# W2 steps take the block stored first, and the emission clock counts PSUM banks

## The chip, the cores and the metric

One core of a Trainium2 chip. The metric is the device time of one execution in microseconds (us). Ratios are the mean time of one kernel's fast runs over that of the other's fast runs of the same rounds, so they are not quite the ratio of the medians quoted beside them.

## The reference, cut to what matters

Two layers; each adds a sliding-window attention and a gated feed-forward block to x (2048 rows of 1024):

```python
x = x + attention(layernorm(x), wqkv, wo)          # 32 heads, 8 keys at distance 2
h = silu(layernorm(x) @ w1) * (layernorm(x) @ w3)  # 3584 columns
x = x + h @ w2
# both lines twice, with the same weights
```

## The kernel before: the parts concerned

The work is cut in eight units: layer, and chunk of 512 rows. The first two units compute the feed-forward block plainly. From the third on, w1, w3 and w2 products use a scheme of seven half-size products, P1 to P7, in place of eight. It needs sums of weight blocks. ScalarE copies and scales four blocks, VectorE makes three more by additions and subtractions, POOL stores all seven to DRAM; there are two blocks for this, 0 and 1, in the buffer `big`. There are two blocks for this, in one buffer (`big`).

```python
big = const.tile([P, 7168], FP16, name="big")
sums = big[:, 0:3072]...                      # norm sums of the activations, for P5, P6, P3
snaps = [big[:, 3072 + 1024 * i: ...]...]     # four snapshots of products
blocks = [big[:, 3584 * i:3584 * (i + 1)]... for i in range(2)]   # block 0 lies over sums
```

A step for W2, as the program is written out (`yield "blocked"` puts the step off):

```python
def sums_of_w2(i, f, ws, loaded):
    a = f % 2
    while "at" not in got2 or pending[a]:
        yield "blocked"
    pending[a] += 1
    ...  # four ScalarE copies into block a; four VectorE operations; pending[a] -= 1; POOL stores block a
    stored[a] = now["dve"] + 7.0
```

The order of instructions on every engine is fixed while the program is written out, by a clock that estimates when each engine gets to what. Fill-in work is put in where the clock says that there is room:

```python
def act_background():                      # ScalarE's fill-in: norms, sizes, sums
    for queue in (acts, sizes, parts, reads):
        while True:
            s = head(queue)
            if s is None or max(now["act"], s[1]) + s[0] > now["pe"] + gate[0]:   # gate is 2.2 us
                break
            take_act(queue)
```

Of the kernel before, what the change touches and what calls it, by code (L numbers as in the profile page):

```python
# [17 lines left out]
def kernel(  # L18
# [137 lines left out]
    opened = [0]  # L156

    def side_tile(*args, **kw):

        while opened[0]:  # L160
            assert head(makes) is not None
            take(makes)
        return side.tile(*args, **kw)

    def bank(name):
        if name == "po":
            return side_tile([P, 512], FP32, name=name, tag="sd")
        return psum.tile([P, 512], FP32, name=name, tag="mm")
# [49 lines left out]
    size_v = const.tile([P, 4], FP32, name="size_v")  # L218
    down_v = const.tile([P, 1], FP32, name="down_v")
    up_v = const.tile([P, 1], FP32, name="up_v")  # L220
# [6 lines left out]
    blocks += [hT[:, 9:16, :].bitcast(FP16).rearrange("p b (k c) -> p b k c", k=KT // 2)]  # L227
    t2_d = [dram.tile([P, 7, (b - a) // 2, 512], FP16, name=f"t2_d{i}") for i, (a, b) in enumerate(fsplits)]
    t_d = [[dram.tile([P, 14, KT // 2, P], FP16, name=f"t_d{m}_{g}") for g in range(NG)] for m in range(2)]
    t_d += [[dram.tile([P, 14, KT // 2, P], FP16, name=f"t_dv_{g}") for g in range(2)]]  # L230
# [350 lines left out]
    def score_steps():  # L581

        V = nc.vector
        for g, (l, h) in enumerate(halves):
# [20 lines left out]
            def gather_heads(t, parts_=parts_):  # L605
                at["L"] = L = side_tile([P, W, BLK], FP32, name="L", tag="sd")
                for i in range(parts_):
                    for a in range(4):
                        nc.tensor.matmul(L[32 * a:32 * (a + 1), :, :], lhsT=gather[:],
                                         rhs=psm[:, :, i, a * BLK:(a + 1) * BLK], start=i == 0, stop=i == parts_ - 1,  # L610
                                         skip_group_check=True)
                at["t"] = pe(1.5 * parts_, t) + 0.2
# [19 lines left out]
            def exps():  # L632
                V.tensor_tensor(L[:], L[:], mx[:].unsqueeze(1).to_broadcast([P, W, BLK]), op=ALU.subtract)
                nc.scalar.activation(E[:], L[:], ACTF.Exp, scale=scale)
                at["E"] = act(0.65, now["dve"] + 0.1, "exp")

# [123 lines left out]
    def o_tile():  # L760
# [12 lines left out]
        for hh in range(2):  # L773
            ps = bank("po")
            for t in range(KT):
                nc.tensor.matmul(ps[:], lhsT=oT[:, t, j * P:(j + 1) * P], rhs=wo[:, t, hh * 512:(hh + 1) * 512],  # L776
                                 start=(t == 0), stop=(t == KT - 1))
            r = pe(KT, oT_at[l, h] + 0.2)
            xs = x_sb[:, n, hh * 512:(hh + 1) * 512]
            background(r)  # L780
            nc.vector.tensor_tensor(xs, xs, ps[:], op=ALU.add)  # L781
            dve(0.64, r)
# [42 lines left out]
    def q_part(l, c, which, ws, then=()):  # L825
# [8 lines left out]
        for t0 in range(0, KT, SG):  # L834
# [3 lines left out]
            for t in range(t0, t0 + SG):  # L838
                ps = bank("ps")
                for kk in range(KT):  # L840
                    nc.tensor.matmul(ps[:], lhsT=ws[kk // KH][:, kk % KH, t::KT], rhs=xnT[:, kk, :],  # L841
                                     start=(kk == 0), stop=(kk == KT - 1))
# [4 lines left out]
                if first:  # L847
                    nc.scalar.copy(kT[:, t, HALO:], ps[:, 0:TCH])
                    done = act(0.3)
                if t < t0 + SG - 1:  # L850
                    pe_requests(2)
            nc.sync.dma_start(qkv_d[l][which][:, t0:t0 + SG, c * CH:(c + 1) * CH], sgt)
            landed = dma(256, done)
            if l == 0:
                stored[0:2] = landed, landed
# [47 lines left out]
    def weight_sums(m, g, w, got):  # L903
# [4 lines left out]
        for a in range(2):  # L908
# [9 lines left out]
            makes.append([differences(m, g, a, a, now["act"] + 0.1), None])  # L918
        made.add((m, g))

    pending, stored, made, held = [0] * 3, [0.0] * 3, set(), []
    junk = hsum[:].bitcast(BF16).rearrange("p k t -> p (k t)")

    def differences(m, g, a, slot, r):

        b = blocks[slot]
# [3 lines left out]
        pending[slot] -= 1  # L930
        nc.gpsimd.dma_start(t_d[m][g][:, 4 * a:4 * (a + 1)], b[:, 0:4])
        nc.gpsimd.dma_start(t_d[m][g][:, 8 + 3 * a:8 + 3 * (a + 1)], b[:, 4:7])
        stored[slot] = now["dve"] + 7.0

    got_v = {}

    def size_of_v(i, w):

        w_ = w[:].rearrange("p k c -> p (k c)")
        half = w_.shape[1] // 2  # L940
        for j in range(2):
            yield 1.95, 40.0, lambda: nc.scalar.activation(junk, w_[:, j * half:(j + 1) * half], ACTF.Square,
                                                           accum_out=size_v[:, 2 * i + j:2 * i + j + 1])
        if i == 1:
            total_scale(size_v, up_v, down_v, got_v)

    def sums_of_v(ws):

        while "at" not in got_v or norm_left.get(("Q", 0, NCH - 1), 1):
            yield "blocked"  # L950
        for g in range(2):
            for a in range(2):
                while pending[2]:
                    yield "blocked"
                pending[2] += 1
                b = blocks[2]
                for i, (kh, fh) in ((0, (0, 0)), (1, (0, 1)), (3, (1, 0)), (5, (1, 1))):
                    t = 4 * g + 2 * fh + a
                    yield 0.61, max(got_v["at"], stored[2]) + 1.0, lambda: nc.scalar.activation(
                        b[:, i], ws[kh][:, :, t::KT], ACTF.Copy, scale=up_v[:])  # L960
                makes.append([differences(2, g, a, 2, now["act"] + 1.0), None])
        made.add("v")
# [72 lines left out]
    def sums_of_w2(i, f, ws, loaded):  # L1035

        a = f % 2
        while "at" not in got2 or pending[a]:
            yield "blocked"
        pending[a] += 1  # L1040
# [28 lines left out]
    def pipeline(key, groups, consume, done, last, fill=None):  # L1069
# [6 lines left out]
        def acc():  # L1076
            return psum.tile([P, 2, HT], FP32, name="st", tag="mm")
# [12 lines left out]
        def head_part(i, name):  # L1090
            G = groups[i]
            s5, su, s22 = snaps[i % 2], snaps[2], snaps[3]
            if name == "P1":
                G["early"] = weight("early")
                G["A"] = acc()
                r = run(G, name, G["A"], True)
                G["B"] = acc()
                nc.scalar.copy(G["B"][:], G["A"][:])  # L1098
                G["tB"] = act(0.5, r)
            elif name == "P5":  # L1100
                G["D"] = acc()
                r = run(G, name, G["D"], True)
# [9 lines left out]
            elif name == "P2":  # L1112
                r = run(G, name, G["B"], False, G["tB"])
                release(1)
                consume(G, 0, G["B"][:], r)
# [11 lines left out]
            elif name == "P3":  # L1127
                r = run(G, name, G["D"], False, G["tD"])
                consume(G, 1, G["D"][:], r)
            else:  # L1130
                r = run(G, name, G["A"], False, G["tC"])
                release(1)
                consume(G, 2, G["A"][:], r)
# [19 lines left out]

    def v_products(l, c):

        key = ("Q", l, c)
        slots, landed = [0], []

        def stage(G, pair):
            if ("to", pair) not in G:  # L1160
                i = slots[0] % 8 * SG
                slots[0] += 1
                G["to", pair] = hT[:, i:i + SG, :]
                G["left", pair] = 2
            return G["to", pair]

        def consume(G, q, src, r):
            pair, t0 = q % 2, HT * (q // 2)
            to = stage(G, pair)
            if q != 3:  # L1170
                nc.scalar.activation(to[:, :, t0:t0 + HT], src, ACTF.Copy, scale=down_v[:])
                r = act(0.57, r)
            G["left", pair] -= 1
            G["at", pair] = max(r, G.get(("at", pair), 0.0))
            if not G["left", pair]:
                t = 4 * G["g"] + 2 * pair
                nc.sync.dma_start(qkv_d[l][2][:, t:t + SG, c * CH:(c + 1) * CH], to)
                landed.append(dma(256, G["at", pair]))
                if len(landed) == 4:
                    qkv_at[l, c, 2] = max(landed)  # L1180

        groups = []
        for g in range(2):
            G = dict(m=2, g=g, inv=down_v[:])
            G["corner"] = lambda G=G: stage(G, 1)[:, :, HT:CH]
            groups.append(G)
        pipeline(key, groups, consume, lambda i: between(False, i == 0), True)
        xnT_free[key] = now["pe"]

    def products(u, f0, f1, hold):  # L1190
# [25 lines left out]
        def output(j, hh, src, r):  # L1216
# [4 lines left out]
            dve(0.69, r)  # L1221
            if l == 1 and lastsplit:
                nc.sync.dma_start(xout[:, n, hh * 512:(hh + 1) * 512], xs)
                dma(128, now["dve"])

        def W(name, j):
# [12 lines left out]
            if name == "P1":  # L1239
                G["A"] = bank("w2")  # L1240
                r = G["1"] = matmuls(G["A"], True)
                G["B"] = bank("w2")
                nc.scalar.copy(G["B"][:], G["A"][:])
                G["tB"] = act(0.5, r)
            elif name == "P2":
                r = G["2"] = matmuls(G["B"], False, G["tB"])
                output(j, 0, G["B"][:], r)
            elif name == "P5":
                G["D"] = bank("w2")
                r = matmuls(G["D"], True)  # L1250
# [15 lines left out]
            elif name == "P3":  # L1266
                r = matmuls(G["D"], False, G["tD"])
                output(j, 1, G["D"][:], r)
            else:
                r = matmuls(G["A"], False, G["tC"])  # L1270
                output(2 + j, 0, G["A"][:], r)
# [20 lines left out]
        def consume(G, q, src, r):  # L1292
            m, g, f = G["m"], G["g"], G["f"] + 2 * (q % 2)
            inv = G["inv"]
            if m == 0:
                sg = gates[g, q] = sgp.tile([P, 2, HT], BF16, name="sg", tag="sg")
                nc.scalar.activation(sg[:], src, ACTF.Silu, scale=inv)  # L1297
                G["t", q] = act(0.6, r, "silu")
            else:
                if q != 3:  # L1300
                    up = tight[:, 1] if q == 2 else sgp.tile([P, 2, HT], BF16, name="up", tag="up", bufs=1)[:]
                    nc.scalar.activation(up, src, ACTF.Copy, scale=inv)
                    src, r = up, act(0.5, r)
                background(r + 0.5)
                t0 = HT * (q // 2)
                nc.vector.tensor_tensor(h16[:, f:f + 2, t0:t0 + HT], src, gates[g, q][:], op=ALU.mult)
                dve(0.34, r)

# [14 lines left out]
    def b_stage(u, hold):  # L1323
# [5 lines left out]
        for (f0, f1) in fsplits:  # L1329
# [4 lines left out]
            for g0 in range(f0, f1, FG):  # L1334
# [3 lines left out]
                for fi in range(gn):  # L1338
# [8 lines left out]
                    pg = bank("pg")  # L1347
                    for kk in range(KT):
# [5 lines left out]
                    ts = act(0.5, r, "silu")  # L1354
                    act_background()
                    pu = bank("pu")
                    for kk in range(KT):
# [5 lines left out]
                    th = dve(0.64, r)  # L1363
                    release_held(2)
# [9 lines left out]
            for hh in range(2):  # L1374
                now["pe"] = max(now["pe"], *times[hh])
                for j in range(TPC):
                    n, step = c * TPC + j, TPC * hh + j
                    acc = psum.tile([P, 512], FP32, name="acc", tag="mm")
# [13 lines left out]
                    dve(0.64, r)  # L1392
# [6 lines left out]
        if u == TU - 1:  # L1399
            force(makes, lambda: not any(pending[0:2]))  # L1400
# [82 lines left out]
```

## Time and profile before

| | before |
|---|---|
| time, median of 3 (4 at the second reading) | 1542.65 us (1542.95) |
| TensorE busy, of the span | 1521.5 of 1542.1 us |
| sum of TensorE's waits in the profile | 14.5 us |
| half-clock stretch of TensorE inside the run | 3.4 us, at 569.4 |

The lines that carry this are in the prediction.

### The profile page before, as it was taken

How to read it: one execution, taken by the hardware profiler on the slowest of the kernel's cores; microseconds unless marked ns; L12 is line 12 of the kernel's file. 1: busy time of each engine (PE TensorE's matmuls, PEld its weight loads, DVE VectorE, ACT ScalarE, POOL GpSimd, SP SyncE). 2: the span in 40 equal slices, each digit the busy share in tenths (PEclk: the TensorE clock that was granted, in tenths of full speed). 3: DMA queues.
4: the chain of work that ended last, by engine and by line, in shares of the span. 5: the costliest groups of instructions: out<-in, count | busy, mean ns of one | idle time of the engine just before them, and what ended most of it. 6: DMA issues, size and time to landing. Idle time of an engine off the chain costs nothing.

```text
span 1542.1 us, 25098 instructions
## 1 busy us (share of the span) xinstructions
PE 1521.5 (99%) x9595; PEld 990.2 (64%) x9634; DVE 1200.9 (78%) x2126; ACT 884.8 (57%) x1388; POOL 156.8 (10%) x308
## 2 busy tenths in 40 slices
PE   9999999999999999999999999999999999999999
PEld 7666644444444567675685756867677667686865
DVE  4689998889979678989898958799688986445345
ACT  3885476667465346555574554666557345554633
POOL 1210102121111100102101010010202000000000
PEclk9999999999999999999999999999999999999999
DMA  9887969798896899969879888798979988878885
GB/s 326 192 230 211 271 209 337 266 307 268 270 307 226 289 326 316 313 236 312 294 285 310 310 282 270 268 342 295 308 259 322 347 281 285 311 273 333 313 295 205
DMA packets 261433, 439.57 MB, mean 285 GB/s; under 512 B 73856, under 2 KB 201088, under 8 KB 245056
## 3 DMA queue, kind: packets, MB, share of 16 engines
q1 hardware_dynamic: 248464, 390.90, 77.2%
q0 software_dynamic: 12704, 46.93, 8.7%
q8 instruction: 75, 1.23, 0.3%
q14 instruction: 46, 0.38, 0.1%
q10 hardware_dynamic: 144, 0.13, 0.0%
HBM read 345.90 MB, written 67.90 MB: 268 GB/s over the span
## 4 chain that ended last, share of the span: by engine, by line
PE 55%; DVE 4%; DMA 3%; ACT 3%; issue 1%; POOL 1%; ACTq 0%; DVEq 0%; POOLq 0%
PE st L1086 29%; PE w L1235 15%; PE ps L841 6%; PE po L776 4%; DMA qkv_d<-hT 1%; DMA t_d<-big 1%; DMA kT<-qkv_d 1%; DVE tree L595 1%; DMA xnT<-xn 1%; DVE tree L515 1%; ACT sg L1297 0%; DVE tree L670 0%; ACT big L1043 0%; ACT xn L323 0%; ACT L1297 0%
## 5 line engine op out<-in xcount | busy, mean ns | idle before, releaser
L841 PE MATMUL ps<-xnT,wqkv 128*128 128x512 f16 (+1 forms) x1469 | 320.7, 379 | 3.1 <-ACT hT L845 1.8
L1086 PEld LDWEIGHTS <-early 128*128 128x128 f16 x2688 | 263.1, 98 | 39.9 <-DVE big L303 1.7
L841 PEld LDWEIGHTS <-wqkv 128*128 128x128 bf16 x1472 | 210.6, 144 | 111.6 <-issue 4.0
L1235 PE MATMUL w<-t,hT 128*128 128x512 f16 x1008 | 226.3, 379 | 1.5 <-ACT big L1255 1.2
L1086 PEld LDWEIGHTS <-late 128*128 128x128 f16 x2016 | 197.4, 98 | 33.8 <-issue 5.5
L595 DVE TENSOR_TENSOR tree<-qT,kT 128x2048 bf16<-128x2048 bf16 x128 | 156.2, 1221 | 29.0 <-DMA qT<-qkv_d 15.4
L670 DVE TENSOR_TENSOR tree<-At,vT 128x2048 bf16<-128x2048 bf16 x128 | 156.1, 1220 | 26.8 <-DMA At<-E 25.2
L515 DVE TENSOR_TENSOR tree<-tree 128x1024 bf16<-128x1024 bf16 x256 | 175.2, 685 | 0.9
L1086 PE MATMUL st<-big,early 128*128 128x256 f16 x1344 | 172.8, 273 | 1.9 <-DVE big L303 1.4
L1086 PE MATMUL st<-xnT,late 128*128 128x256 f16 x1344 | 174.2, 273 | 0.2
L1235 PEld LDWEIGHTS <-hT 128*128 128x128 f16 x1008 | 98.3, 98 | 113.6 <-issue 3.1
L1086 PE MATMUL st<-xnT,early 128*128 128x256 f16 x1344 | 165.3, 273 | 0.0
L1098 ACT COPY st<-st 128x512 f32<-128x512 f32 x84 | 48.3, 575 | 119.6 <-PE st L1086 118.8
L776 PE MATMUL po<-wo,oT 128*128 128x512 bf16 x487 | 111.6, 379 | 2.9 <-DVE x_sb L781 1.6
L1358 PE MATMUL pu<-xnT,w3t 128*128 128x512 f16 x448 | 105.8, 379 | 0.0
L1349 PE MATMUL pg<-xnT,w1t 128*128 128x512 f16 x448 | 105.8, 379 | 0.0
L1380 PE MATMUL acc<-w2t,hT 128*128 128x512 bf16 x437 | 97.8, 379 | 0.6
L1110 DVE TENSOR_TENSOR st<-st,big 128x512 f32<-128x512 f32 x84 | 58.4, 695 | 50.2 <-ACT big L1107 50.1
L845 ACT CAST hT<-ps 128x512 bf16<-128x512 f32 x96 | 54.9, 586 | 71.3 <-PE ps L841 70.2
L1297 ACT ACTIVATE sg<-st,down_scale 128x512 bf16<-128x512 f32 x126 | 86.7, 688 | 12.6 <-PE st L1086 12.1
L1086 PE MATMUL st<-big,late 128*128 128x256 f16 x672 | 87.9, 274 | 3.8 <-DVE st L1110 3.8
L776 PEld LDWEIGHTS <-oT 128*128 128x128 bf16 x512 | 50.0, 98 | 58.3 <-issue 2.6
(167 smaller groups left out, 1919.3 us busy)
## 6 DMA issues: line engine op xcount, KB each, us to landing
early<-t_d SPq DMA_DIRECT2D x84, 1024.0 KB, 6.9
late<-t_d SPq DMA_DIRECT2D x84, 768.0 KB, 6.4
t<-t_d SPq DMA_DIRECT2D x42, 1024.0 KB, 7.6
t<-t_d SPq DMA_DIRECT2D x42, 768.0 KB, 5.3
wqkv<-in_A_wqkv_dram SPq DMA_DIRECT2D x28, 1024.0 KB, 9.0
w1t<-in_B_w_dram SPq DMA_DIRECT2D x14, 1024.0 KB, 8.0
w3t<-in_B_w_dram SPq DMA_DIRECT2D x14, 1024.0 KB, 10.9
t_d<-big POOLq DMA_DIRECT2D x28, 512.0 KB, 6.0
```

Source lines behind the costliest of these rows:

```text
L515: nc.vector.tensor_tensor(b, b, buf[:, 4:8, :], op=ALU.add)
L595: V.tensor_tensor(pr, qT[:], kT[:, :, k0:k0 + TCH], op=ALU.mult)
L670: V.tensor_tensor(tm.rearrange("p w (a e) -> p w a e", a=4), At[:].rearrange("p a w e -> p w a e"), win, op=ALU.mult)
L776: nc.tensor.matmul(ps[:], lhsT=oT[:, t, j * P:(j + 1) * P], rhs=wo[:, t, hh * 512:(hh + 1) * 512], start=(t == 0), stop=(t == KT - 1))
L841: nc.tensor.matmul(ps[:], lhsT=ws[kk // KH][:, kk % KH, t::KT], rhs=xnT[:, kk, :], start=(kk == 0), stop=(kk == KT - 1))
L1086: nc.tensor.matmul(out[:, a, :], lhsT=w[:, a, blk, k, :], rhs=rhs[:, k, :], start=start and a == 0 and k == 0, stop=k == KQ - 1, skip_grou ...
L1110: nc.vector.tensor_tensor(G["D"][:], G["D"][:], su, op=ALU.add)
L1235: nc.tensor.matmul(out[:], lhsT=lhs[:, k, j * P:(j + 1) * P], rhs=w[:, k, :], start=start and k == 0, stop=k == nq - 1, skip_group_check=True)
L1297: nc.scalar.activation(sg[:], src, ACTF.Silu, scale=inv)
L1349: nc.tensor.matmul(pg[:], lhsT=w1t[:, kk, fi * P:(fi + 1) * P], rhs=xnT[:, kk, :], start=(kk == 0), stop=(kk == KT - 1))
L1358: nc.tensor.matmul(pu[:], lhsT=w3t[:, kk, fi * P:(fi + 1) * P], rhs=xnT[:, kk, :], start=(kk == 0), stop=(kk == KT - 1))
L1380: nc.tensor.matmul(acc[:], lhsT=hT[:, f, j * P:(j + 1) * P], rhs=tiles[hh][f // nq][:, f % nq, :], start=(f == 0), stop=(f == f1 - f0 - 1))
```

## The change

Intent: a W2 step should not wait for the block whose store was issued last when the other is free. The emission clock should also know when TensorE has to wait for a PSUM bank (the place in PSUM that a group of matmuls writes its result to; the tiles of this kernel take six of them in turn, and two for side work), so that fill-in work is placed by a truer clock. Code for v products that nothing calls goes out. The core:

```diff
-        a = f % 2
-        while "at" not in got2 or pending[a]:
+        while "at" not in got2 or all(pending):
             yield "blocked"
+        a = min((i for i in range(2) if not pending[i]), key=lambda i: stored[i])
...
+    rings = dict(mm=[], sd=[])
+    def turn(tag, bufs):
+        ring = rings[tag]
+        if len(ring) >= bufs:
+            now["pe"] = max(now["pe"], ring[-bufs])
+        ring.append(0.0)
+        return ring, len(ring) - 1
+    def free(at, t):
+        ring, i = at
+        ring[i] = t + 0.1
...
-            return psum.tile([P, 2, HT], FP32, name="st", tag="mm")
+            return mm_tile([P, 2, HT], "st")          # takes a turn first
...
-                consume(G, 2, G["A"][:], r)
+                free(G["A@"], consume(G, 2, G["A"][:], r))
```

(cut: the same turn and free for the other tiles, and the removal of the v products)

## The prediction

> **What bounds the kernel now.** I read the page's busy lines first, then TensorE's own waits, then the chain of waits around the longest of them, and last the timelines of ScalarE and of the load queue there.
>
> ```profile
> PE 1521.5 (99%) x9595; PEld 990.2 (64%) x9634; DVE 1200.9 (78%) x2126; ACT 884.8 (57%) x1388; POOL 156.8 (10%) x308
> ...
> PE st L1086 <- DVE st L1110: 3.8, 1, 3.8
> PE ps L841 <- ACT hT L845: 1.8, 1, 1.8
> PE po L776 <- DVE x_sb L781: 1.6, 2, 0.8
> PE st L1086 <- DVE big L303: 1.4, 1, 1.4
> PE w L1235 <- ACT big L1255: 1.2, 2, 0.7
> PE ps L841 <- DMA wqkv<-in_A_wqkv_dram: 1.2, 2, 1.0
> ```
>
> TensorE is busy 1521.5 of 1542.1 us, so at most 20.6 us lie outside its work. Is "busy" also full speed here? The chain of waits holds runs such as 8 matmuls of 512 columns in 1.73 us, 0.216 us each, again and again, so yes. The waits (us in total, times, longest) are eleven rows, 14.5 us together; the six shown are 11.0 of it. A change of order can win only from these. The three of 3.8, 1.8 and 1.0 us all fall between 525 and 570 us, where the kernel leaves its plain B stages and makes q, k, v of the second layer. The chain there:
>
> ```profile
> 506.43 8.89 DMA t_d<-big
> 515.32 3.69 ACT big L1043 x6
> ...
> 519.40 4.32 DMA t_d<-big
> ...
> 524.46 1.93 ACT big L1043 x3
> 526.39 0.96 ACT hT L845 x2
> ...
> 527.37 14.60 DMA qkv_d<-hT
> ...
> 541.99 12.42 DMA kT<-qkv_d
> ...
> 569.30 0.62 DVE st L1110
> 569.92 0.04 issue
> 569.96 10.04 PE st L1086 x78
> ```
>
> (start, us, what.) One path runs from the store of a block of weight sums through the W2 steps (L1043), the evacuation of q, its store, the load of kT and VectorE's score trees to the vector addition TensorE stood 3.8 us for. So these waits have one root: ScalarE came to the W2 steps late. Its timeline, and that of the load queue:
>
> ```profile
> 513.99 5.01 ACT L1043 ACTIVATE big<-w2t,up 128x512 f16<-128x512 bf16 x8 [19.08 <-DMA wqkv<-in_A_wqkv_dram]
> 523.83 2.56 ACT L1043 ACTIVATE big<-w2t,up 128x512 f16<-128x512 bf16 x4 [4.83 <-DMA t_d<-big]
> 526.30 3.48 ACT L845 CAST hT<-ps 128x512 bf16<-128x512 f32 x7
> ...
> 524.58 2.27 SPq L712 DMA_DIRECT2D wqkv<-in_A_wqkv_dram  x4
> ```
>
> ScalarE sat idle 19.1 us before the first W2 step and 4.8 us before the third. The label of the first wait is a load, but the L1043 copies write a block of sums and read W2 tiles long in use by TensorE; the chain, which names the store of sums, is right.
>
> **What the Trainium skill says.** *TensorE: Matmul & The Clock Gate*, "Architectural detail": ScalarE's and VectorE's queues are strict FIFO. The trace agrees: seven evacuations of ps sit directly behind the last W2 step at 526.30, though TensorE had been filling the banks since 514. *PSUM — Partial Sum Buffer*, "Specifications": a bank holds 512 FP32 values, so every 128x512 f32 tile here is a whole bank, and the pool of six is six banks; TensorE got through 48 matmuls (six tiles of eight, 514.15 to 525.1) and stopped. *DMA: Bandwidth & Descriptors*, "Issuing engines are not separate DMA queues" (with the key constraint of the skill's front page): all issuing queues share 16 DMA engines. The trace agrees: the store of a whole block takes 4.3 us at 519, but that of half a block takes 8.9 us at 506, where xnT transposes and wqkv loads run beside it.
>
> **Part 1, the block that a W2 step takes.** Before, step f takes block f mod 2 and waits if it is pending. The weight sums before it always use block 0, then block 1, so block 0's store goes first. Four runs of W2 steps exist: f = 0-3, 0-2, 4-7, 3-5. Three begin at an even f, with block 0, as the change would choose. Only the last (f = 3, at 514 us) begins with block 1, the store issued later. The change makes it block 0, 1, 0. So this part moves about 3 of 14 steps; no instruction is added.
>
> Block 0's second store was issued at 499.91 us, block 1's at 506.43 (POOL's timeline). Giving block 0 the slow 8.9 us, it is free at 508.8; with the page's median of 6.0 us, at 505.9. A step is four copies, 2.56 us. Slow case: step one ends at 511.4. From the end of step one's copies to the landing of its store took 7.2 us before (516.55 to 523.73), so step three starts at 518.6 and ends at 521.1. Quick case: step two, behind block 1, ends at 516.6 at the earliest and step three at 519.2. Before it ended at 526.39. ScalarE is free **5 to 7 us earlier**. What follows:
> - The evacuation comes before the sixth bank is full at 525.1: the 1.8 us wait goes.
> - The load queue stood 9.4 us behind L1043 (its own waits) until 524.58, since W2 tiles hold the slots of the next weights. Four 1 MB loads go out about 5 us earlier, and the 1.0 us wait for wqkv at 531 goes. Together some 3 us.
> - The 3.8 us wait at 566. It ends when kT lands (554.4) plus 15 us of VectorE trees queued ahead of L1110. The windows view has the DMA engines at 0.38 busy from 515 to 520 and at 0.93 to 1.14 from 535 to 560; earlier loads fill the hole, worth about 0.6 x 5 = 3 us. But qT and kT are issued behind the q stores, which follow TensorE's own pace. So I let kT, the trees and L1110 move 3 to 5 us, **4 us** as the middle (an estimate). TensorE itself comes 3 us earlier to that wait, so most of it stays: the region ends 4 us earlier, not 7.
>
> **Part 2, the emission clock counts banks.** The order of instructions is fixed when the program is written out, by a clock that estimates each engine. It is now pushed on when TensorE would wait for a bank. No instruction is added, removed or lengthened; the order of fill-in work may move. What real waits would it have known? Only those on an evacuation: 1.8 us (ps) and 1.6 us (two po tiles, 0.8 each). The other 11 us are loads, snapshots and vector additions, of which the clock already knew the engine part. With part 1 the 1.8 us is gone as well. So the pushes are about 2 us in 1542, and they do not free a bank; they only let background work be placed a little later or more of it. I count **0, with a scatter of 3 us either way**: after 570 us about 8 us of small waits remain (1.4 behind L303, 1.2 behind L1255, 0.9 on a score tree), and a moved VectorE step can remove or add one such.
>
> **Part 3, the v products and their block.** Nothing calls them in the program as it stands (q_part does all three of q, k, v), so removing them is worth 0. Norms are still looked at ahead of weight sums, as before.
>
> Sum: 1542.65 - 4 - 0 = about 1538.5; I say **1538.0**, leaning half a microsecond to the side of the change, since the clock of the following stretch is then nearer to the truth.
>
> **Rivals.**
> - The DMA engines are the bound from 525 to 560. For it: busy shares over 1.0 and kT's 12.4 us from issue to landing. Then kT still lands at 554, L1110 still ends at 569.9, and the first two waits simply move into the third: 1542, no gain.
> - The whole path shortens by the 5 to 7 us and the order of trees also turns out better: all of 1.8 + 1.0 + 3.8 goes, 1536; with a po wait and another small one gone, 1533. For it: they are one chain with one root.
> - The new order puts VectorE background ahead of an addition TensorE needs. VectorE is at 94 to 98% in several 50 us stretches before 500 us and TensorE still never waits there, which speaks against a big loss; one new stall of the size of the old one (4 us) would give 1542 to 1546.
> - The W2 sums matter before 500 us too: ScalarE waits 8.4 us at 434. Against: TensorE shows no wait there at all, so that is hidden either way.
>
> **Range and chances.** Most likely 1538; the gain of 4 us has a spread of about 3 from part 1 and 3 from part 2, together 4: 1532.5 to 1543.5 holds it 8 times in 10. Two per cent is 31 us: all TensorE's waits together are half of that, so faster by over 2% is out of reach (0.01), and a loss of 31 us would take eight stalls of the worst size (0.01). Within 2%: 0.98.
>
> **What would show it.** Right: the first L1043 copies of the last run start at 506 to 509 us, the last end by 522; the wait of ps for hT and the wait of 1.0 us for wqkv are gone from TensorE's waits; busy times of all engines unchanged within 1%; TensorE's wait behind L1110 still there, at 2 to 4 us. Wrong: L1043 still starts at 514 (a pending block, not a landing store, held it); kT lands at 554 as before; or a new row of over 2 us in TensorE's waits after 570 us.

## The result, and the profile after

The changed kernel took 1549.49 us (median of 4, 1546.56 to 1551.31) against 1542.95: ratio 1.0039, interval 1.0019 to 1.0059. A second reading (run 5) gave 1547.14 against 1543.84, 1.0023. It is within 2%, but slower, and outside the range predicted.

The page's busy line and TensorE's waits, changed kernel (columns as in the prediction):

```profile
PE 1522.9 (98%) x9594; PEld 989.0 (64%) x9634; DVE 1201.0 (78%) x2126; ACT 883.6 (57%) x1388; POOL 152.4 (10%) x308
...
PE ps L861 <- DMA wqkv<-in_A_wqkv_dram: 5.0, 4, 3.3
PE st L1078 <- ACT big L1102: 3.7, 5, 1.5
PE L L626 <- DVE psm L535: 2.8, 1, 2.8
...
PE ps L861 <- ACT hT L865: 0.6, 1, 0.6
```

The work is the same to 1%. The waits have changed their kind: the 3.8 us behind the vector addition is gone and that for evacuation went from 1.8 to 0.6 us, but loads of wqkv hold TensorE 5.0 us instead of 1.2, and two rows are new. One waits for a score tree (psm: the tree of VectorE's additions that makes the attention scores). The other waits for ScalarE's copy of the sixth product (L1102).

ScalarE's timeline of the last run of W2 steps, changed kernel (start, length, what; idle time before it in brackets):

```profile
497.09 0.72 ACT L1035 ACTIVATE big<-w2t,up 128x512 f16<-128x512 bf16 x1 [2.81 <-DVE mv L265]
498.82 1.33 ACT L1035 ACTIVATE big<-w2t,up 128x512 f16<-128x512 bf16 x2 [1.01 <-DVE big L949]
502.51 0.72 ACT L1035 ACTIVATE big<-w2t,up 128x512 f16<-128x512 bf16 x1 [2.36 <-issue]
...
522.39 2.56 ACT L1035 ACTIVATE big<-w2t,up 128x512 f16<-128x512 bf16 x4 [4.21 <-DMA t_d<-big]
```

The first step did come early: its four copies ran from 497.1 to 503.2 instead of from 514. Yet the third began at 522.4 instead of 523.8. The second step (513.8 to 518.2) is left out here. Between the first step's copies and the third step stand VectorE's four operations on the block and POOL's store of it:

```profile
507.77 1.68 DVE L1041 TENSOR_TENSOR big<-big 128x512 f16<-128x512 f16 x4
509.99 0.91 POOL L1044 DMA_DIRECT2D t_d<-big  x1 [3.60 <-DVE big L1041]
```

By the trace's landing times this store landed at 522.28.

VectorE's first norm sum after the steps, before and then changed:

```profile
528.99 0.68 DVE L303 TENSOR_TENSOR big<-xnT 128x1024 f16<-128x1024 f16 x1
```

```profile
536.21 0.69 DVE L319 TENSOR_TENSOR big<-xnT 128x1024 f16<-128x1024 f16 x1 [8.58 <-DMA t_d<-big]
```

The norm sums (L303, now L319) write the buffer big, and now wait 8.6 us for a store out of it. Before, they ran with no wait.

Windows of ten us, before and then changed (columns: stretch and its length, busy us of PE, PEld, DVE, ACT and POOL with counts, granted clock, DMA share, GB/s):

```profile
515.00:525.00 10.00, 9.80 (x45) 6.37 (x45) 3.82 (x9) 5.17 (x9) 1.81 (x2) 1.00 0.59 205
525.00:535.00 10.00, 7.21 (x33) 4.52 (x32) 8.27 (x20) 5.95 (x12) 0.89 (x1) 1.00 0.95 314
```

```profile
515.00:525.00 10.00, 9.72 (x44) 6.38 (x45) 2.23 (x6) 4.09 (x8) 0.90 (x1) 1.00 1.16 172
525.00:535.00 10.00, 5.18 (x22) 2.88 (x22) 2.46 (x10) 3.92 (x8) 0.89 (x1) 0.91 1.03 384
```

In the first stretch the changed kernel keeps the DMA engines twice as busy and moves no more: 1.16 at 172 GB/s (1.07 at 207 in the second reading) against 0.59 at 205. In the second TensorE loses two us more, and the clock falls below 1. The trace's record of the granted clock has 6.8 us at half clock from 533.2 on, against 3.4 us at 569.4 before. The Trainium skill's *TensorE: Matmul & The Clock Gate*, "What's actually happening", says that the array drops to half clock after an idle window of about 3.4 us. The lengths agree: the half-clock stretches inside these runs are 3.4, 6.8 or 10.2 us long, one to three windows. That the window must be idle throughout does not (see the last section). A window full of matmuls loses half its length, 1.7 us (an estimate); here the 20 matmuls from 534.52 on took 7.19 us, where 20 at 0.216 would take 4.3.

To place the loss, the next table takes the same matmul in two traces (the n-th that writes a tile of the name st, whose order is the same in all) and gives how much later than in the trace of before it starts. Points between 576 and 960 are left out, since the order of the output tiles between them differs.

| kernel (us later than before at) | 559.9 | 575.7 | 961.7 | 1125.0 | 1212.7 | end |
|---|---|---|---|---|---|---|
| changed | 7.6 | 2.3 | 0.0 | 2.2 | 4.6 | 4.0 |
| choice of block alone | 9.3 | 4.0 | 0.8 | 2.7 | 2.7 | 2.8 |
| clock alone | 3.4 | 2.0 | -3.3 | -1.4 | 1.0 | 0.4 |
| clock alone, products do not push | -0.4 | 2.3 | -1.9 | -1.9 | -1.9 | -1.8 |
| changed, sums moved | 6.0 | 0.7 | -1.7 | 1.0 | 3.3 | 2.7 |
| before, sums moved | 1.5 | -2.0 | -2.4 | -2.4 | -2.4 | -2.5 |
| changed, store behind | 11.4 | 6.1 | 3.8 | 6.6 | 9.0 | 8.4 |
| changed, both moves | -1.0 | -3.4 | -5.0 | -3.1 | -0.7 | -1.3 |
| choice alone, both moves | -0.5 | -2.2 | -5.4 | -3.5 | -3.5 | -3.1 |

It is one trace of each kernel, and the first columns are rough: in its second reading the changed kernel is 7.4 and 2.1 us late at the first two points, and the choice of block alone, whose order of instructions is the same up to 612 us, 9.3 and 4.0. The steps from 961.7 to 1212.7 repeat: they are 4.6 and, in the second reading of the changed kernel, 5.3. So there are two places to explain: 505 to 567 us, and 961 to 1213. By 961.7 the changed kernel is level with before. So the first place is where the predicted gain is missing (2.3 us late at 575.7 instead of 4 early), and the second is where the changed kernel falls behind.

### The profile page after: what moved, and what is told of

Its sections match the earlier page's. It is cut to its first block, busy times and chain, and to the rows that moved or that the text cites. A ratio compares the mean times of both kernels' runs of the same rounds, so it can differ in the third digit from the quotient of the medians.

```text
span 1546.1 us, 25093 instructions
## 1 busy us (share of the span) xinstructions
PE 1522.9 (98%) x9594; PEld 989.0 (64%) x9634; DVE 1201.0 (78%) x2126; ACT 883.6 (57%) x1388; POOL 152.4 (10%) x308
## 3 DMA queue, kind: packets, MB, share of 16 engines
q8 instruction: 75, 1.23, 0.3%
## 4 chain that ended last, share of the span: by engine, by line
PE 84%; DVE 8%; DMA 4%; ACT 2%; issue 2%; SPq 0%; ACTq 0%; DVEq 0%; POOLq 0%
PE st L1078 29%; PE ps L861 19%; PE w L1195 14%; PE po L795 7%; PE pg L1316 5%; PE pu L1327 5%; PE acc L1351 3%; DMA t_d<-big 3%; DMA wqkv<-in_A_wqkv_dram 1%; DVE tree L611 1%; DVE tree L531 1%; PE pq L465 1%; DVE tree L688 1%; DVE big L949 0%; PE L L626 0%
## 5 line engine op out<-in xcount | busy, mean ns | idle before, releaser
L861 PE MATMUL ps<-xnT,wqkv 128*128 128x512 f16 (+1 forms) x1469 | 324.1, 382 | 5.7 <-DMA wqkv<-in_A_wqkv_dram 5.0
L1105 DVE TENSOR_TENSOR st<-st,big 128x512 f32<-128x512 f32 x84 | 58.4, 696 | 53.4 <-ACT big L1102 53.3
L1260 ACT ACTIVATE sg<-st,down_scale 128x512 bf16<-128x512 f32 x126 | 86.6, 687 | 11.9 <-PE st L1078 11.4
```

Of the source, the lines that this page charges most:

```text
L861: nc.tensor.matmul(ps[:], lhsT=ws[kk // KH][:, kk % KH, t::KT], rhs=xnT[:, kk, :], start=(kk == 0), stop=(kk == KT - 1))
L1105: nc.vector.tensor_tensor(G["D"][:], G["D"][:], su, op=ALU.add)
L1260: nc.scalar.activation(sg[:], src, ACTF.Silu, scale=inv)
```

## The experiments

Eleven runs, all correct, 5 rounds each. "Before" is the kernel before of the same job: medians 1544.24 (first four runs), 1543.84 (next four), 1543.34 (last three).

**1 and 2. One half of the change at a time.**

```diff
# choice of block alone, in the kernel before        # clock alone, in the changed kernel
-        a = f % 2                                    -        a = min((i for i in range(2) if not ...
+        a = min((i for i in range(2) if not ...      +        a = f % 2
```

> The kernel before with the choice of block for W2 steps alone; the emission clock is the old one. Theory A (the choice of block makes the loss between 505 and 567 us: last run of W2 steps goes 0, 1, 0, its first store runs beside the xnT transposes, and its last block covers the norm sums): slower than before by 3 to 8 us, 1546 to 1551, with the wqkv waits of TensorE at 4 to 5 us near 530 us and VectorE idle some 8 us before the norm sums. Rival B (the new clock's order makes the loss): 1537 to 1543.

> The changed kernel with the old choice of block (step parity). Theory A: no loss at 505 to 567 us, so within 3 us of before, 1540 to 1546; last W2 run goes 1, 0, 1 and the first step waits until 514 us. Rival B (the new clock's order makes the loss): 1547 to 1551, as the changed kernel.

Measured: choice alone 1546.65 us, ratio 1.0012 (0.9998 to 1.0026); clock alone 1546.69, 1.0012 (0.9999 to 1.0024). The choice alone is within theory A's range, but the clock alone is in neither: so neither theory alone is right. The halves cost alike, some 1.9 us of mean time each by the ratios, together about what the whole costs in its second reading (3.6 us). Either alone is not clear of noise. In the traces they cost in different places. The choice alone has the wqkv waits (6.7 us in all between 500 and 580) and the score-tree wait, and is 4.0 us late at 575.7. Of the two, the clock alone has the larger loss from 961 to 1213, 4.3 us against 1.9.

**3 and 4. Where the norm sums lie.** The last run of W2 steps has three. Before, they took blocks 1, 0, 1; now 0, 1, 0. So the last store now leaves from block 0, and block 0 lies over the norm sums. To test this the sums and the snapshots change places; the order of every engine stays the same, row by row.

```diff
-    sums = big[:, 0:3072]            +    sums = big[:, 4096:7168]
-    snaps = big[:, 3072 + 1024*i:]   +    snaps = big[:, 1024*i:]
-    tight = big[:, 6144:7168]        +    tight = big[:, 3072:4096]
```

> The changed kernel with only the place of two things in one buffer swapped: norm sums lie over block 1 and snapshots over block 0. The order of instructions on every engine is the same as in the changed kernel. If the wait of the norm sums for the last store (8.6 us of VectorE) is what costs (theory A1), that wait goes, and so does TensorE's 2.8 us wait for the score tree: 1542 to 1546. If the wqkv loads and the half clock after them are the larger part (theory A2), these stay (4 to 5 us of wait near 530) and the time is only 1 to 3 us under the changed kernel.

> The kernel before with the same swap, order unchanged. Its last W2 step uses block 1, which now covers the norm sums. Theory A1: norm sums wait for the store issued at 528.6 us and landed at 539.0, VectorE idles some 8 to 10 us there, and the kernel slows by 2 to 6 us, to 1545 to 1549. If the place does not matter (A2): within 1 us of before.

Measured: the changed kernel with the sums moved 1546.55 (1.0009), the kernel before with them moved 1541.95 (0.9986). The holds are where the theory puts them. In the changed kernel the norm sums no longer wait and the 2.8 us wait for the score tree is gone; in the kernel before, VectorE now idles 9.96 us until a store lands. Yet the times hardly follow: the first stays slow, with 5.1 us of waits for wqkv and 6.8 us at half clock, and the second did not become slower. It even became faster, if only just clear of noise (interval 0.9974 to 0.9999); in its trace the gain is there by 575.7, the wait for wqkv is gone, and the wait behind L1110 is shorter (1.7 us). No run here tells why. As the whole cause, theory A1 falls.

**5. The changed kernel again** (no edit), for a reading on the same chip as the next three.

> The changed kernel itself once more, on the same chip as the next three and as the kernel before. Expected as at first, 4 to 7 us slower than before. If the two halves add up (choice of block alone and clock alone were each 1.9 us slower), about 4 us.

Measured: 1547.14, ratio 1.0023 (1.0011 to 1.0036), so 3 to 4 us slower.

**6 and 7. The early store beside the transposes.** In the changed kernel POOL issues the first W2 step's store at 509.99 us, while two DMA transposes of xn are in flight (issued from 506.23). By the trace's landing times the store took 12.3 us, and the transposes landed at 523.9 and 524.6; before they landed at 516.2 and 517.1, and W2 stores took 4.3 and 4.9 us. In the packet record the store's packets and those of the transposes mix from 515 to 523, so it did not only stand behind the stores that POOL had issued before it. The edit sends this one store through the load queue, where it stands behind the transposes:

```diff
-            nc.gpsimd.dma_start(t2_d[i][:, :, f, :], b)
+            (nc.sync if (i, f) == (1, 3) else nc.gpsimd).dma_start(t2_d[i][:, :, f, :], b)
```

> The changed kernel with one store (that of the first W2 step of the last run) issued by the load queue, behind the two xnT transposes, instead of by POOL beside them. Order on TensorE, VectorE and ScalarE unchanged. Theory C (the early store and the transposes slow each other: store landed after 12.3 us, transposes 7.5 us later than before): transposes land near 517 us again, the store by 521, the third step starts 1 to 3 us sooner, the wqkv waits of TensorE shrink from 4.7 us to under 2.5, and the time falls by 2 to 6 us against the changed kernel. Rival D (the DMA engines are full from 523 us on whatever goes before): no change of more than 1.5 us.

> The same move of one store in the kernel with the choice of block alone (old clock). Theory C: 2 to 6 us under the choice alone, so 1541 to 1545, at or under before. Rival D: as the choice alone, 1545 to 1548.

Measured: 1549.51 (1.0037) and 1547.11 (1.0022); not a microsecond gained. But theory C's mechanism did show: in the changed kernel with the store behind, the transposes land at 518.0 and 518.9, and the store, issued 7 us later at 517.0, lands at 522.95, no later than when it went early (around 505 this trace runs 2.4 us behind that of the changed kernel). The windows view for 515 to 525 gives 270 GB/s at a share of 0.89, against 172 at 1.16. The second wqkv load lands at 531.9 instead of 534.5. TensorE's waits from 500 to 580 us there:

```profile
PE L L626 <- DVE psm L535: 9.7, 1, 9.7
PE ps L861 <- DMA wqkv<-in_A_wqkv_dram: 0.8, 1, 0.8
```

The loads hold TensorE 0.8 us, and the score tree 9.7 us in one wait (536.5 to 546.2), with 10.2 us at half clock from 540.4 on, 4.4 of them after the wait. TensorE got to the tree's matmul sooner and met the same end: it could go on at 546.2 here, at 544.5 in the changed kernel. So two holds end at nearly the same time, one hidden behind the other. Removing the loads' hold alone (run 6) gained nothing, and removing the tree's alone (run 3) nothing clear of noise: 1.0009, against 1.0039 and 1.0023 of the changed kernel in other jobs.

**8 and 9. Both moves together** (the edits of 3 and 6).

> The changed kernel with both moves: norm sums lie over block 1, and the store of the first W2 step goes behind the xnT transposes. Order on TensorE, VectorE and ScalarE as in the changed kernel. Theory G (two holds end near 544 us and hide each other: wqkv loads pushed back by the store beside the transposes, and the score tree held by the norm sums, which wait for the last store in the block that covers them): with both gone TensorE has no wait over 2 us from 515 to 565, at most one half-clock window, and the time is 1539 to 1543, 4 to 7 us under the changed kernel. Rival H (a third hold behind these, such as kT landing late): 1545 to 1548, and the profile names it.

> The choice of block alone (old clock) with both moves. Against the same with the store moved only (1547.1), only the place of the norm sums differs. Theory G: the 9.6 us wait for the score tree goes, 1538 to 1542, faster than before by 1 to 5 us. Rival H: 1544 to 1547.

Measured: the changed kernel with both moves 1542.97 (1542.57 to 1543.54), ratio 0.9999; choice of block alone with both moves 1540.72 (1540.40 to 1541.39), 0.9985 (0.9972 to 0.9999). Neither profile has a half-clock window inside the run, and five runs lie within 1 us, where those of the changed kernel spread over 2.0 and 4.8 us (two readings) and those of before, nine in this job, over 4.7. TensorE's waits from 500 to 580 us in the changed kernel with both moves:

```profile
PE st L1078 <- DVE st L1105: 2.8, 1, 2.8
PE ps L861 <- DMA wqkv<-in_A_wqkv_dram: 1.4, 2, 1.1
```

Theory G holds in its main part: both holds gone, the time 4 to 6.5 us down (against other jobs). Its "no wait over 2 us from 515 to 565" held only to the letter: the wait for the vector addition, which the prediction had found in the kernel before (3.8 us), is back at 2.8, from 565.2 on, so rival H has a small share. And the table shows that the stretch to 575.7 now gains on the kernel before.

**10. Pushes by the products' tiles.** For the loss from 961 to 1213, the clock alone, where tiles of the seven-product scheme (names st and w2) take their turns but no longer push:

```diff
-        if len(ring) >= bufs:
+        if push and len(ring) >= bufs:
...
-        turns["mm"] = turn("mm", 6)
+        turns["mm"] = turn("mm", 6, name not in ("st", "w2"))
```

> The new clock alone (old choice of block), but tiles of the products pipeline and of its W2 part no longer push the clock; q, k, v, gate, up, W2 and output tiles still do. One push of 2.2 us near 525 us is all that is left of it by a run of the emission. Theory E (pushes by the products' tiles let ScalarE's fill-in be placed ahead of the copies TensorE waits for): the waits behind the copy of the sixth product vanish and the stretch from 961 to 1213 us takes as long as before (within 0.5 us; with all pushes it took 4.3 us more). Rival F (any reordering from 525 us on moves those waits at random): the stretch stays 2 us or more longer.

Measured: 1542.05, ratio 0.9992 (0.9980 to 1.0005), against 1.0012 with all pushes. TensorE's waits from 961 to 1213 us, clock alone, and then without these pushes:

```profile
PE st L1078 <- ACT big L1102: 2.3, 3, 1.5
PE w L1195 <- ACT big L1218: 0.4, 1, 0.4
```

```profile
PE w L1195 <- ACT sg L1260: 0.3, 1, 0.3
```

The waits behind L1102 vanish, and the stretch takes as long as before (0.0 us more instead of 4.3). Theory E is right for this stretch. Rival F keeps a share: the choice of block alone pushes nothing, and its other order alone costs 1.9 us from 961 to 1125.

What such a wait looks like: ScalarE's timeline of the changed kernel around 1189 us, then the same place before.

```profile
1188.23 0.68 ACT L1260 ACTIVATE sg<-st,down_scale 128x512 bf16<-128x512 f32 x1
1188.80 1.23 ACT L366 ACTIVATE xn<-x_sb,mom 128x1024 f16<-128x1024 bf16 x1
1189.93 0.57 ACT L1102 COPY big<-st 128x512 f32<-128x512 f32 x1
```

```profile
1184.74 0.68 ACT L1297 ACTIVATE sg<-st,down_scale 128x512 bf16<-128x512 f32 x1
1185.31 0.58 ACT L1107 COPY big<-st 128x512 f32<-128x512 f32 x1
1185.78 0.71 ACT L1297 ACTIVATE sg<-st,down_scale 128x512 bf16<-128x512 f32 x1
1186.70 1.24 ACT L350 ACTIVATE xn<-x_sb,mom 128x1024 f16<-128x1024 bf16 x1 [0.21 <-POOL mom L333]
```

A norm (xn, 1.23 us), which nobody waits for at this moment, now stands ahead of the copy that TensorE needs for the next product; TensorE waits 1.5 us. Before, it stood two places behind it.

**11. A candidate for a better kernel:** the edits of 10 and 3, with the old choice of block.

> The clock without pushes by products' tiles and the old choice of block, with norm sums moved over block 1 (last store is then block 1). A candidate for a kernel better than both: the clock alone without these pushes gave 0.9992 of before, the move in before gave 0.9986. If the two add up: 1540 to 1542. If the later norm sums hold the score tree here: 1543 to 1546.

Measured: 1540.71 (1539.74 to 1541.61), 0.9985 (0.9972 to 0.9997). It ties with the choice of block alone with both moves: both beat the kernel before of their job by about 2.3 us. So did the kernel before with nothing but the norm sums moved (run 4, 0.9986). So no run here shows that the choice of block gains anything beyond that move. Its trace shows a 4.5 us wait for the score tree near 545, the hold by the norm sums again, yet it ends 2.7 us ahead of before. So part of this gain is in the order after 575 us (4.3 us up to 961), which no run here takes apart.

## Why the prediction was wrong

- **What bounds the kernel: right.** The work stayed the same to 1%, TensorE's waits decided, and a 2% change was out of reach.
- **"Step one ends at 511.4": right in kind.** It ended at 503.2, sooner still: block 0's second store took 3.1 us, not 6.0 or 8.9, and the copies could take the parts of the block one by one as they were stored.
- **"From the end of step one's copies to the landing of its store took 7.2 us before, so step three starts at 518.6 and ends at 521.1": this step failed.** It took 19.1 us, from 503.2 to 522.28. VectorE's four operations stood in its queue until 507.8, and the store took 12.3 us beside the transposes instead of the 4.3 that the 7.2 contains. The prediction had shown that stores are slower in this company (8.9 us at 506) and then moved a store into that company at the price of a quiet one. ScalarE came free at 524.9, 1.4 us sooner instead of 5 to 7.
- **"Four 1 MB loads go out about 5 us earlier": failed with it.** They went out 1.4 us earlier, into DMA engines still busy with the slowed transposes, and the second landed 2.2 us later (534.5 against 532.3). The wait for wqkv grew from 1.2 to 5.0 us.
- **"kT, the trees and L1110 move 3 to 5 us": kT did, by luck, the rest did not.** kT landed at 549.2 instead of 554.4, though it was issued later (543.64 against 541.99): it took 5.6 us instead of 12.4. The addition (L1110, now L1105) started at 572.63 instead of 569.22, and TensorE, later still, no longer waits for it.
- **"These waits have one root": not so.** In run 4 ScalarE comes to the W2 steps as late as before (513.75 and 523.61), yet the wait for wqkv is gone and that behind L1110 is 1.7 us instead of 3.8 (one trace).
- **What the prediction left out: the place of the last store.** It worked out that the blocks become 0, 1, 0 and did not ask what else lies over block 0. The norm sums do, so they and the score tree behind them were held until the last store landed. In the kernel before the same kind of hold cost TensorE 1.1 us (run 4); there TensorE has 120 matmuls of q, k, v ahead of the tree's matmul, in the changed kernel 88 (counts of the timelines), so it arrives some 7 us sooner (32 matmuls at 0.216, an estimate) and has to wait.
- **Left out too: the half clock.** The prediction asked whether "busy" was full speed and said yes from some runs of the chain. At the end of the long wait in the kernel before came 3.4 us at half clock. So a hold of a few us can cost more than its length, by up to 1.7 us a window. That such windows also make the runs scatter is not shown; the two kernels without any scatter least.
- **"The pushes are about 2 us in 1542 ... I count 0": wrong in size and sign.** It counted the bank waits in the trace. The clock pushes on its own estimates: printed while the changed program is written out (these are no times of the chip), there are 38 pushes, 14.1 us in all, 5.6 of them in the stretch of the late loss and none before 566. With the choice of block in place, switching off the products' pushes gives exactly the order of the choice alone (the two programs compared, instruction by instruction), so the two kernels with both moves differ by these pushes only: 1542.97 against 1540.72, so they cost 2.2 us. Why they overshoot was only argued: fill-in may be taken until ScalarE stands 2.2 us ahead of TensorE in the clock; then banks look free late, TensorE's clock is pushed on, and that makes room for more fill-in.
- **The rivals.** "The DMA engines are the bound from 525 to 560" and "VectorE background ahead of an addition TensorE needs" came nearest, but both missed (and "94 to 98% in several 50 us stretches" holds for two before 500 us): the new loads' wait begins with what ran from 510 to 525, and the fill-in that hurt was ScalarE's.
- **What would show it wrong** had named "a new row of over 2 us after 570 us", and the row for L1102 (3.7 us in five pieces) is it.

Still open: how much of the order's effect between 575 and 961 us (gains of 2 to 5 us in several variants) belongs to which move.

## What to carry to other kernels

Before letting work take whichever buffer is free first, ask what else lies in that buffer's bytes and who needs them next, and whether its transfer will then run beside one that it slows. When one removed wait gives no time, look for a second hold that ends at the same moment, and remove both in one run. A clock that places fill-in by its own estimate of stalls must not use that stall to place more fill-in ahead of what the stalled engine waits for.

## What the Trainium skill lacked or had wrong

- *DMA: Bandwidth & Descriptors*, "Rules for kernel authors", says that a transpose next to ordinary DMAs needs nothing. That is for correct data; the page has no figure for the speed of the two together. Here a 0.9 MB store beside two transposes took 12.3 us, and the transposes landed some 7 us later than without it; sent after them, the store took 5.9 us and landed no later. Yet at 499.9 in the kernel before a 0.4 MB store beside two transposes took 3.2 us and they 4.0 to 4.3, so what it takes for them to slow each other stays open.
- *TensorE: Matmul & The Clock Gate*, "HAM oscillation", gives "no PE-idle gaps >~3.4µs" as the rule. Here one wait of 2.0 us (the kernel before with sums moved, at 524) was followed by a half-clock window (TensorE was busy for 1.42 of the 3.40 us before it), and one of 3.4 us (choice alone with both moves, at 565) by none, so the length of a wait alone does not tell.
